# Turning fourteen far tiles of a fused attention backward by DMA, in fixed tiles

## The chip, the cores and the metric

The kernel runs on one core of a Trainium2 chip. The metric is the time of one execution of the whole program in microseconds of the device. Of the core's engines five appear below: TensorE (PE) multiplies matrices and turns (transposes) tiles, VectorE (DVE), ScalarE (ACT) and GpSimd (POOL) work on elements, and SyncE (SP) here does nothing but issue DMA transfers. Each engine works through its own list of instructions in order, and they wait for one another by semaphores.

## The reference: a gated mix of attention and a gated FFN, forward and backward

For a sequence x of 2048 tokens of width 512 the reference computes

```python
g = sigmoid((x * gate_w).sum(-1, keepdims=True))
a = attention(x, wqkv, wo)          # 32 heads of 16, causal, window of 256 keys
b = reglu_ffn(x, W_gate, W_up, W_down)   # inner width 1376
out = g * a + (1 - g) * b
```

and the gradients of `out` against a given `grad_out`, with respect to x as the attention and the gate see it, wqkv, wo, the three FFN weights and gate_w. The input of the FFN is a constant of its own for the gradient. In attention a query i sees the keys k with 0 <= i - k < 256: with tokens cut into blocks of 128, the queries of block j meet the key blocks j (diagonal, cut by the causal mask), j-1 (whole) and j-2 (cut by the far edge of the window). Everything is in bf16, with sums in float32.

## The kernel before

**Stages.** The FFN comes first, forward and backward (to about 249 us). Then comes attention, forward and backward together, in four head groups c = 0 to 3 of eight heads each; in the profiled execution they start at about 249, 351, 467 and 583 us. The output stage follows from about 713 us: a loop over 16 token tiles that makes b (`bps`, L1030) and dwo, and from 767 us a second loop over the 16 tiles that makes a (`aps`, L1064), out and dx (`dxps`, L1055 and L1085).

**A unit of attention.** A head group has 16 rows j (128 queries each). A row has up to three key blocks: "d" (block j), "m" (j-1) and "f" (far, j-2), and each is done in two halves of four heads. So a full row has six units, in the order m, f, d for half 0 and m, d, f for half 1, and the whole has 360. A unit goes through these steps:

- `front`: scores `ST` (L688, keys on the partitions, 128x512), the exp on ACT (L697) into `Pu`, and for d and f a mask on POOL (L699, L702);
- `front_dp`: `dPT` (L711), the product of V and the incoming gradient;
- `gradp`: `Pd = Pu * dPT` on DVE (L716);
- `rowsum`: 8 matmuls (L725, L727) that sum outputs, row sums and dQ of the row in one PSUM tile `BA`;
- `flip`: `Pu` and `Pd` turned, so that queries lie on the partitions, 8 blocks of 128x128;
- `cd_piece`: 8 matmuls (L542, L545) from the turned tile into `CD`, the dK and dV of one key block; when the last piece of a key block is in, ACT copies `CD` out (L548).

**Two ways to turn.** For d and m the two halves share a tile (`PPd`, `PPm`, three buffers each) and are turned together by one DMA transpose of 16 blocks on SP (L744) into `p2d` or `p2m`. The far units are turned one by one by 8 PE transposes (L754) into PSUM, from where ACT (L72) or DVE (L74) copies them into SBUF, by turns. The far tiles `Pu` and `Pd` have two buffers each, the turned ones four.

**The order of work.** One loop over slots n writes the instructions of all engines, and each engine keeps that order. Slot n does `front` of unit n, `front_dp` of unit n-1, `gradp` of unit n-2, the DMA turning of unit n-3 where there is one, and with LAG = 4 `rowsum` of unit n-4 and its PE turning. Pieces of `CD` stand in a queue `cdq` with the slot from which they may go: n+1 for earlier rows, n+5 for the newest row. A credit, refilled each slot and lowered by what PE is given, lets background work in: the projections Q, K, V, dO of the next four rows (`project_parts`, whose `rows` are one 8-block DMA transpose, L181), and the weight gradient of the head group before (`grad_parts`: four parts of four steps of four matmuls, L642; each part's result is stored by SP). All four parts of a head group are released at row 3 of the next one.

**Late turns.** The output stage needs wqkv, W_gate and W_up turned. `turns` cuts them into DMA transposes of up to 8 blocks on SP (L582). They go into slots of SBUF that earlier work has left: x0 to x3, d0 to d3, p0 to p3, each 128 x 4 x 512; p0 to p3 held the projection weights of the four head groups. The table `plan` says after which group of projections which turns may go; they then leave a list `late` one at a time, in head groups 1 and 2 at the slots with n % 12 == 1 in rows 3 to 8. What is in `W_rest` goes in the output stage: four at its start, and then one at each pair of token tiles of the `bps` loop. In the seventh pair `load_wo` and `load_b(0)` follow on SP: W_o, `dgT_g`, `duT_g` and the DMA transpose `turned` (L840), which `aps` reads. `clear` zeroes, on POOL, the 32 rows of a last weight tile that the weight doesn't fill.

Of the kernel before, what the change touches and what calls it, by code (L numbers as in the profile page):

```python
# [11 lines left out]
BF = mybir.dt.bfloat16  # L12
# [10 lines left out]
def kernel(  # L23
# [74 lines left out]
    def slot(tag):  # L98
        return big.tile([P, DC, TGW], BF, tag=tag, name=tag)
# [415 lines left out]
    if True:  # L515
# [68 lines left out]
        def clear(name):  # L584
            nc.gpsimd.memset(W6[(name, FC - 1)][0:FC * P - F, :], 0.0)
# [8 lines left out]
        def turns(name, src, k0, k1, tag):  # L594
            full, end = src.shape[1] // P, -(-src.shape[1] // P)
            ks = range(k0, min(k1, full))
            sets = [list(ks[i:i + 2]) for i in range(0, len(ks), 2)] + ([[full]] if k0 <= full < min(k1, end) else [])
            return [lambda s=s: turn_w(name, src, s, tag, s[0] - k0) for s in sets]
# [19 lines left out]
        def load_gw():  # L618
            nc.sync.dma_start(gw_b[:], gate_w.partition_broadcast(P))

        plan = {2: [load_gw], 5: turns("wqkv", A_wqkv, 0, 4, "p0"), 7: turns("wqkv", A_wqkv, 4, 8, "p1"),
                11: turns("wqkv", A_wqkv, 8, 12, "p2"),
                12: turns("Wg", B_W_gate, 0, 4, "x0") + turns("Wg", B_W_gate, 4, 8, "d0"),
                13: loads("Wd", B_W_down, 0, "x1") + loads("Wd", B_W_down, 4, "d1"), 14: loads("Wd", B_W_down, 8, "x2")}
        W_rest = (turns("Wg", B_W_gate, 8, 12, "d2") + [lambda: clear("Wg")] + turns("Wu", B_W_up, 0, 4, "x3") + turns("Wu", B_W_up, 4, 8, "d3")
                  + turns("Wu", B_W_up, 8, 12, "p3") + [lambda: clear("Wu")])

        def grad_parts(c, tail=False):
            out = []
# [26 lines left out]
                    out.append((lambda part=part, t0=t0, f=(t0 == 0), l=(t0 + 4 == NT): piece(part, t0, f, l), t0 + 4 < NT))  # L656
            return out

        class Unit:
            pass  # L660

        units = []
        for c in range(DC):
            for j in range(NT):
                kbs = [k for k in (j - 1, j, j - 2) if k >= 0]
                for half in range(2):
                    order = kbs if half or len(kbs) < 3 else [kbs[0], kbs[2], kbs[1]]
                    for ki, kb in enumerate(order):
                        u = Unit()
                        u.c, u.j, u.kb, u.half = c, j, kb, half  # L670
                        u.first = ki == 0 and half == 0
                        u.last = ki == len(kbs) - 1 and half == 1
                        u.role = ("d", "m", "f")[j - kb]
                        u.pair = u.role == "d" or (u.role == "m" and (c < DC - 1 or j < NT - 2))
                        u.own = u.role == "f"
                        u.dma = u.pair
                        units.append(u)
        NU = len(units)

        pairs = {}  # L680

        def front(u):
            tg, jl = u.j // TPG, u.j % TPG
            z = zt[(u.c * NTG + tg) % ZB]
            KTt = proj[(u.c, u.kb // TPG)][f"K{u.half}"]
            ksl = slice((u.kb % TPG) * P, (u.kb % TPG + 1) * P)
            ST = ps.tile([P, HH, P], F32, tag="M", bufs=4, name="ST")
            nc.tensor.matmul(ST[:], lhsT=KTt[:, ksl], rhs=z[:, 0, :, jl, :], start=True, stop=True)  # L688
            if not u.own:
                if u.half == 0:  # L690
                    tag = f"PP{u.role}"
                    pairs[(u.c, u.j, u.kb)] = wk.tile([P, 2, 2, HH, P], BF, tag=tag, bufs=3, name=tag)
                u.PP = pairs[(u.c, u.j, u.kb)][:, u.half, :, :, :]
                u.Pu, u.Pd = u.PP[:, 0, :, :], u.PP[:, 1, :, :]
            else:
                u.Pu = wk.tile([P, HH, P], BF, tag="Pu", bufs=2, name="Pu")
            nc.scalar.activation(u.Pu[:], ST[:], ACT.Exp)  # L697
            if u.role == "d":
                nc.gpsimd.affine_select(out=u.Pu[:], in_=u.Pu[:], compare_op=ALU.is_ge, fill=0.0, base=0,  # L699
                                        pattern=[[0, HH], [1, P]], channel_multiplier=-1)  # L700
            elif u.role == "f":
                nc.gpsimd.affine_select(out=u.Pu[:], in_=u.Pu[:], compare_op=ALU.is_ge, fill=0.0, base=-1,  # L702
                                        pattern=[[0, HH], [-1, P]], channel_multiplier=1)
# [7 lines left out]
            nc.tensor.matmul(u.dPT[:], lhsT=VTt[:, ksl], rhs=z[:, 1, :, jl, :], start=True, stop=True)  # L711

        def gradp(u):
            if u.own:
                u.Pd = wk.tile([P, HH, P], BF, tag="Pd", bufs=2, name="Pd")
            nc.vector.tensor_tensor(out=u.Pd[:], in0=u.Pu[:], in1=u.dPT[:], op=ALU.mult)  # L716

        def rowsum(u):
# [17 lines left out]
        def flip(u):  # L736
            key = (u.c, u.j, u.kb, "p2")
            if u.role != "f" and key not in P2 and not (u.pair and u.half == 0):
                P2[key] = wk.tile([P, 2, 2, HH, P], BF, tag=f"P2{u.role}", bufs=3, name=f"p2{u.role}")
            if u.dma:  # L740
                if u.pair and u.half == 0:
                    return
                hs = slice(0, 2) if u.pair else slice(u.half, u.half + 1)
                nc.sync.dma_start_transpose(out=P2[key][:, hs, :, :, :].rearrange("p b a h q -> p (b a h) q"),  # L744
                                            in_=pairs[(u.c, u.j, u.kb)][:, hs, :, :, :].rearrange("p b a h q -> p (b a h q)"))
                for b in range(2)[hs]:
                    P2[(u.c, u.j, u.kb, b)] = P2[key][:, b, :, :, :]
                return
            eng = ("act", "dve", "act")[copier["i"] % 3] if u.c == 0 else ("act", "dve")[copier["i"] % 2]
            copier["i"] += 1  # L750
            pt = psr.tile([P, 2, HH, P], BF, tag="TR", name="pt")
            for a, src in enumerate((u.Pu, u.Pd)):
                for hh in range(HH):
                    nc.tensor.transpose(pt[:, a, hh, :], src[:, hh, :], ident[:])  # L754
            p2 = P2[key][:, u.half, :, :, :] if u.role == "m" else wk.tile([P, 2, HH, P], BF, tag="P2f", bufs=4, name="p2")[:]
            evac(p2, pt[:], eng)
            P2[(u.c, u.j, u.kb, u.half)] = p2

# [84 lines left out]
        with tc.manual_schedule():  # L843
# [36 lines left out]
            while n <= NU + LAG or ev or cdq or bgq:  # L880
                now = ev.pop(n, [])
                u = units[n] if n < NU else None
                if u is not None:
                    gi = u.c * NTG + u.j // TPG
                    if u.first and u.j == 0:
                        sts[u.c] = st.tile([P, NT, 4, P], BF, tag="rows_st", name="rows_st")
                    if u.first and u.j % TPG == 0:
                        if gi + 1 < len(groups):
                            prq = project_parts(*groups[gi + 1]) if gi else second
                            due = n + sum(2 * min(3, j + 1) for j in range(u.j, u.j + TPG)) - 3  # L890
                            if gi + 2 == len(groups):
                                due -= 10
                    if u.first and u.j == TPG and ends:
                        copies.append(ends.pop(0))
                    if u.first and u.j == 1 and u.c > 0:
                        ready = grad_parts(u.c - 1)
                    if u.first and u.j == TPG - 1 and u.c > 0:
                        bgq += ready
                    front(u)
                    if u.last and gi + 1 == len(groups) and u.j % TPG in (1, 3):  # L900
                        ev.setdefault(n + 2, []).append(("dma", (lambda: load_a(0)) if u.j % TPG == 3 else lambda: load_h(0)))
# [18 lines left out]
                if w is not None:  # L920
                    rowsum(w)
                    if not w.dma:
                        flip(w)
                    if w.last:
                        for s, eng, f in small_ops(w.c, w.j, n - 2):
                            ev.setdefault(s, []).append((eng, f))
                        done = [w.j - 2] if w.j >= 2 else []
                        if w.j == NT - 1:
                            done += [NT - 2, NT - 1]
                        for kb in done:  # L930
                            qbs = range(kb, min(NT, kb + 3))
                            for qb in qbs:
                                for half in range(2):
                                    e = n + (1 if qb < w.j else 5)
                                    cdq.append((e, w.c, kb, qb, half, qb == qbs[-1] and half == 1))
                if v is not None and not (w is not None and w.first):
                    front_dp(v)
# [29 lines left out]
                if u is not None and u.c == DC - 1 and not bgq and u.j > 6 and "grads" not in S2:  # L967
                    S2["grads"] = grad_parts(DC - 1, True)
                calm = not NU - 8 < n < NU + 3
                if late and calm and (u is None or u.c == 0 or (n % 12 == 1 and 3 <= u.j <= 8 if u.c < DC - 1 else  # L970
                                                       n % 4 == 1 and 1 < u.j < 10 or n % 2 and u.j > 9)):
                    late.pop(0)()
                credit = max(-1.0, min(1.2, credit))
# [179 lines left out]
```

## Time and profile before

| | us |
|---|---|
| median of 3 runs (lowest to highest) | 905.12 (904.67 to 905.77) |
| the profiled execution | 905.65 |
| its span, first to last instruction | 903.9 |
| attention, head groups 0 / 1 / 2 / 3 | 101.9 / 115.5 / 115.9 / 130.4 |
| output stage, first / second loop | 54.0 / 136.9 |
| busy: PE / DVE / POOL / ACT | 884.3 / 510.0 / 493.7 / 445.6 |

The profile takes one execution. Its span runs from the first to the last instruction. "Busy" counts the time in which an engine had at least one instruction running. The granted TensorE clock was 0.999 of full speed. Lines of a timeline give the start, the duration, the engine and the line of the kernel, and the operation with its output and inputs by the program's names; on an engine's queue (SPq) the duration is the time that the issue of a DMA took, and its landing is a later event. PE's matmuls overlap, so the distance between starts is what one costs. The chain of waits follows the work that ended last back to what released each step. The three kinds of turnings in numbers: 928 PE transposes (L754), 122 DMA transposes of pairs (L744), 16 of `rows` (L181).

### The profile page before, as it was taken

The numbers are of one execution on the slowest core, as the hardware profiler recorded it, in microseconds if no ns is written. First come the engines' busy times: TensorE is split into PE (matmuls) and PEld (weight loads), VectorE is DVE, ScalarE is ACT, GpSimd is POOL, SyncE is SP. The second block draws the span as 40 slices with busy tenths as digits, with TensorE's granted clock in tenths as the row PEclk, the third lists the DMA queues.
The fourth block names the chain that finished last, engine by engine and source line by source line (L and its number), as shares of the span: only waits on it lengthen the run. The fifth ranks groups of instructions, "written<-read, shape, count | busy, mean of one in ns | idle before, by whom it ended". The sixth has DMA issues, their size and how long they took to land.

```text
span 903.9 us, 25852 instructions
## 1 busy us (share of the span) xinstructions
PE 884.3 (98%) x10507; PEld 560.5 (62%) x10607; DVE 510.0 (56%) x946; ACT 445.6 (49%) x787; POOL 493.7 (55%) x937
## 2 busy tenths in 40 slices
PE   8999999999989999999999999999999999999998
PEld 5556656555657777667776677766767644444445
DVE  4433344335368887678886778876777101333343
ACT  6422232222278777667776677766778212111111
POOL 4644445445267778767877577876678200222232
PEclk9999999999999999999999999999999999999999
DMA  9988889999789999999999989999999999998930
GB/s 302 202 191 190 192 181 214 212 215 214 191 138 159 189 184 192 186 176 156 179 181 185 186 161 187 177 198 181 212 178 189 243 248 220 268 273 225 206 117 30
DMA packets 520983, 174.57 MB, mean 193 GB/s; under 512 B 446816, under 2 KB 519744, under 8 KB 520864
## 3 DMA queue, kind: packets, MB, share of 16 engines
q1 hardware_dynamic: 498624, 150.62, 89.6%
q10 hardware_dynamic: 20608, 17.70, 7.2%
q0 software_dynamic: 1632, 4.59, 1.5%
q8 instruction: 83, 1.36, 0.6%
q14 instruction: 36, 0.29, 0.1%
HBM read 34.37 MB, written 36.24 MB: 78 GB/s over the span
## 4 chain that ended last, share of the span: by engine, by line
PE 83%; DVE 5%; DMA 4%; ACT 3%; issue 2%; POOL 2%; SPq 1%; ACTq 0%; POOLq 0%; DVEq 0%
PE dxps L1055 8%; PE ST L688 7%; PE dPT L711 7%; PE wps L412 7%; PE pt L754 5%; PE wps L642 5%; PE dxps L1085 4%; PE bps L1030 4%; PE CD L542 4%; PE BA L725 4%; PE dhps L363 4%; PE pp L133 3%; PE gps L363 3%; PE dps L414 3%; PE ups L363 3%; PE CD L545 3%
## 5 line engine op out<-in xcount | busy, mean ns | idle before, releaser
L688 PE MATMUL ST<-z,K 128*128 128x512 bf16 x360 | 135.8, 378 | 4.5 <-ACT PPd L697 1.3
L711 PE MATMUL dPT<-z,V 128*128 128x512 bf16 x360 | 135.9, 378 | 1.9 <-DVE Pd L716 0.6
L699 POOL TENSOR_SCALAR_AFFINE_SELECT PPd<-PPd 128x512 bf16<-128x512 bf16 x128 | 81.7, 639 | 80.6 <-ACT PPd L697 80.3
L377 POOL TENSOR_TENSOR hT<-rg,upm 128x512 bf16<-128x512 bf16 x44 | 51.7, 1175 | 113.5 <-DVE upm L375 96.8
L412 PE MATMUL wps<-dgu_r,x_r 128*128 128x256 bf16 (+1 forms) x704 | 103.9, 270 | 1.4 <-DVE wst L74 0.6
L716 DVE TENSOR_TENSOR PPd<-PPd,dPT 128x512 bf16<-128x512 bf16 x128 | 86.9, 679 | 20.5 <-PE dPT L711 12.9
L702 POOL TENSOR_SCALAR_AFFINE_SELECT Pu<-Pu 128x512 bf16<-128x512 bf16 x112 | 72.3, 646 | 34.9 <-ACT Pu L697 33.8
L697 ACT ACTIVATE PPd<-ST 128x512 bf16<-128x512 f32 x128 | 77.0, 603 | 24.6 <-PE ST L688 18.7
L716 DVE TENSOR_TENSOR Pd<-Pu,dPT 128x512 bf16<-128x512 bf16 x112 | 76.4, 682 | 21.2 <-PE dPT L711 11.0
L412 PEld LDWEIGHTS <-x_r 128*128 128x128 bf16 x704 | 68.4, 98 | 31.7 <-issue 1.1
L697 ACT ACTIVATE Pu<-ST 128x512 bf16<-128x512 f32 x112 | 67.4, 602 | 37.0 <-PE ST L688 36.8
L716 DVE TENSOR_TENSOR PPm<-PPm,dPT 128x512 bf16<-128x512 bf16 x120 | 80.1, 667 | 7.1 <-PE dPT L711 5.9
L697 ACT ACTIVATE PPm<-ST 128x512 bf16<-128x512 f32 x120 | 72.4, 603 | 16.8 <-PE ST L688 16.3
L375 DVE SCALAR_TENSOR_TENSOR upm<-rg,ups 128x512 bf16<-128x512 bf16 x44 | 30.1, 685 | 80.0 <-PE ups L363 38.7
L369 ACT ACTIVATE rg<-gps 128x512 bf16<-128x512 f32 x44 | 26.3, 598 | 88.0 <-PE gps L363 47.9
L1067 ACT COPY a_sb<-aps 128x512 f32<-128x512 f32 x16 | 9.4, 586 | 107.2 <-issue 99.8
L72 ACT COPY p<-pt 128x1024 bf16<-128x1024 bf16 x59 | 60.1, 1019 | 4.2
L414 PE MATMUL dps<-db_r,h_r 128*128 128x512 bf16 x159 | 60.3, 379 | 0.0
L387 POOL TENSOR_TENSOR dgu<-dh_sb,rg 128x512 bf16<-128x512 bf16 x44 | 57.2, 1301 | 5.3 <-ACT dh_sb L383 5.3
L642 PE MATMUL wps<-rows_st,x_r 128*128 128x384 bf16 x256 | 50.3, 325 | 0.0
L386 DVE TENSOR_TENSOR dgu<-dh_sb,upm 128x512 bf16<-128x512 bf16 x44 | 32.4, 737 | 27.4 <-ACT dh_sb L383 25.2
L133 PE MATMUL pp<-x,p 128*128 128x512 bf16 x152 | 44.4, 378 | 1.9
(179 smaller groups left out, 2315.9 us busy)
## 6 DMA issues: line engine op xcount, KB each, us to landing
dqkvo_d<-rows_st SPq DMA_DIRECT2D x15, 512.0 KB, 3.8
hT_d<-hT ACTq DMA_DIRECT2D x44, 128.0 KB, 2.7
dgT_d<-dgu ACTq DMA_DIRECT2D x44, 128.0 KB, 3.0
duT_d<-dgu ACTq DMA_DIRECT2D x44, 128.0 KB, 3.0
h<-hT_d SPq DMA_DIRECT2D x8, 640.0 KB, 5.7
dgT_g<-dgT_d SPq DMA_DIRECT2D x8, 640.0 KB, 5.5
duT_g<-duT_d SPq DMA_DIRECT2D x8, 640.0 KB, 6.5
go_g<-in_grad_out_dram SPq DMA_DIRECT2D x16, 256.0 KB, 4.9
```

What stands on the lines that cost most here:

```text
L133: nc.tensor.matmul(pp[:], lhsT=w_p[c][:, cd, which * P:(which + 1) * P], rhs=x_T[tg][:, cd, :], start=(cd == 0), stop=(cd == DC - 1))
L363: nc.tensor.matmul(out[:], lhsT=w(c), rhs=x(c), start=(c == 0), stop=(c == DC - 1))
L412: nc.tensor.matmul(acc["w"][:, c, 0:2 * nw], lhsT=x_r[:, t, c * P:(c + 1) * P], rhs=k.dgu_r[:, :, i, s0:P], start=(go_ and c % 2 == 0), st ...
L414: nc.tensor.matmul(acc["d"][:], lhsT=k.h_r[:, i, :], rhs=db_r[:, t, :], start=go_, stop=no_)
L642: nc.tensor.matmul(wps[:], lhsT=x_r[:, t, part * P:(part + 1) * P], rhs=sts[c][:, t, 0:3, :], start=first and t == t0, stop=last and t == ...
L688: nc.tensor.matmul(ST[:], lhsT=KTt[:, ksl], rhs=z[:, 0, :, jl, :], start=True, stop=True)
L697: nc.scalar.activation(u.Pu[:], ST[:], ACT.Exp)
L699: nc.gpsimd.affine_select(out=u.Pu[:], in_=u.Pu[:], compare_op=ALU.is_ge, fill=0.0, base=0, pattern=[[0, HH], [1, P]], channel_multiplier=-1)
L702: nc.gpsimd.affine_select(out=u.Pu[:], in_=u.Pu[:], compare_op=ALU.is_ge, fill=0.0, base=-1, pattern=[[0, HH], [-1, P]], channel_multiplier=1)
L711: nc.tensor.matmul(u.dPT[:], lhsT=VTt[:, ksl], rhs=z[:, 1, :, jl, :], start=True, stop=True)
L716: nc.vector.tensor_tensor(out=u.Pd[:], in0=u.Pu[:], in1=u.dPT[:], op=ALU.mult)
L1055: nc.tensor.matmul(to, lhsT=src[:, fc, lsl], rhs=W6[(wt, fc)][:, cols], start=(fc == 0 and wt == "Wg"), stop=False)
```

## The change

- Fourteen far units, those of half 0 in rows 3, 4, 5, 6, 8, 9 and 10 of head groups 1 and 2, are turned by a DMA transpose of 8 blocks on SP, issued like the pairs in slot n+3, instead of by PE.
- For that, `Pu` and `Pd` of every far unit now lie in one tile `PF`. The far tiles are eight in fixed assignment by row and half: `PF` (two) and `P2F` (four, turned), and in head groups 1 and 2 one more of each in the slot p0.
- Since p0 is in use for longer, the two turns of the first wqkv columns into it move from the plan (after projection group 5) to the end of `W_rest`, so to the output stage. `clear("Wu")` becomes part of the last turn of W_up.
- In head groups 1 and 2 the `CD` pieces of the newest row may go from slot n+7 on, not n+5.
- In head groups 1 and 2 one part of the weight gradient is released at each of the rows 3, 6, 10 and 14.
- In head groups 1 and 2 the late turns go at the first unit of rows 7 and 11.

```diff
-        plan = {2: [load_gw], 5: turns("wqkv", A_wqkv, 0, 4, "p0"), 7: turns("wqkv", A_wqkv, 4, 8, "p1"),
+        plan = {2: [load_gw], 7: turns("wqkv", A_wqkv, 4, 8, "p1"),
...
-                  + turns("Wu", B_W_up, 8, 12, "p3") + [lambda: clear("Wu")])
+                  + turns("Wu", B_W_up, 8, 12, "p3"))
+        W_rest[-1] = lambda last=W_rest[-1]: (last(), clear("Wu"))
+        W_rest += turns("wqkv", A_wqkv, 0, 4, "p0")
...
+        FARC = (1, 2)
...
-                        u.dma = u.pair
+                        u.far = u.own and half == 0 and c in FARC and j in (3, 4, 5, 6, 8, 9, 10)
+                        u.dma = u.pair or u.far
...
+        PF = [wk.tile([P, 2, HH, P], BF, tag=f"PF{i}", bufs=1, name="PF")[:] for i in range(2)]
+        P2F = [wk.tile([P, 2, HH, P], BF, tag=f"P2f{i}", bufs=1, name="p2f")[:] for i in range(4)]
+        far = {}
+
+        def far_tile(u, turned):
+            if u.c not in FARC:
+                return P2F[(2 * u.j + u.half) % 4] if turned else PF[u.half]
+            if not far:
+                x = slot("p0")[:].rearrange("p k n -> p (k n)")
+                far["x"] = [x[:, i * 1024:(i + 1) * 1024].rearrange("p (a h q) -> p a h q", a=2, h=HH) for i in range(2)]
+            if not turned:
+                return PF[1] if u.half else (PF[0], far["x"][0])[u.j % 2]
+            return P2F[2 + u.j % 2] if u.half else (P2F[0], P2F[1], far["x"][1])[u.j % 3]
...
-                u.Pu = wk.tile([P, HH, P], BF, tag="Pu", bufs=2, name="Pu")
+                u.PP = far_tile(u, False)
+                u.Pu, u.Pd = u.PP[:, 0, :, :], u.PP[:, 1, :, :]
...
+            if u.far:
+                P2[(u.c, u.j, u.kb, u.half)] = p2 = far_tile(u, True)
+                nc.sync.dma_start_transpose(out=p2.rearrange("p a h q -> p (a h) q"),
+                                            in_=u.PP.rearrange("p a h q -> p (a h q)"))
+                return
...
-            p2 = P2[key][:, u.half, :, :, :] if u.role == "m" else wk.tile([P, 2, HH, P], BF, tag="P2f", bufs=4, name="p2")[:]
+            p2 = P2[key][:, u.half, :, :, :] if u.role == "m" else far_tile(u, True)
...
-                    if u.first and u.j == TPG - 1 and u.c > 0:
+                    if u.first and u.c in FARC and u.j in (3, 6, 10, 14):
+                        bgq += ready[:NT // 4]
+                        del ready[:NT // 4]
+                    if u.first and u.c > FARC[-1] and u.j == TPG - 1:
                         bgq += ready
...
-                                    e = n + (1 if qb < w.j else 5)
+                                    e = n + (1 if qb < w.j else 7 if w.c in FARC else 5)
...
-                if late and calm and (u is None or u.c == 0 or (n % 12 == 1 and 3 <= u.j <= 8 if u.c < DC - 1 else
+                if late and calm and (u is None or u.c == 0 or (u.first and u.j in (7, 11) if u.c < DC - 1 else
```

More of the change, by code (lines that the diff above doesn't have):

```diff
@@ L713, in gradp @@
         def gradp(u):
-            if u.own:
-                u.Pd = wk.tile([P, HH, P], BF, tag="Pd", bufs=2, name="Pd")
             nc.vector.tensor_tensor(out=u.Pd[:], in0=u.Pu[:], in1=u.dPT[:], op=ALU.mult)
```

## The prediction
> **What bounds the kernel now.** I read the page first, then TensorE's groups and timeline, then SyncE's (SP) timeline, then the chain of waits in the last attention head group, and last the hand-over to the output stage.
>
> The page:
>
> ```profile
> PE 884.3 (98%) x10507; PEld 560.5 (62%) x10607; DVE 510.0 (56%) x946; ACT 445.6 (49%) x787; POOL 493.7 (55%) x937
> ...
> q1 hardware_dynamic: 498624, 150.62, 89.6%
> ...
> PE 83%; DVE 5%; DMA 4%; ACT 3%; issue 2%; POOL 2%; SPq 1%; ACTq 0%; POOLq 0%; DVEq 0%
> ```
>
> TensorE is the bound nearly everywhere, and SP's queue (q1) is busy 89.6% of the span. So a saving on PE counts in full only while the queue, which is to do the work instead, has room.
>
> What one turning on PE costs, in the timeline (start, duration, instruction):
>
> ```profile
> 402.39 0.38 PE L754 MATMUL pt<-ident,Pu 128*128 128x128 bf16 x4
> 402.61 0.39 PE L754 MATMUL pt<-ident,Pd 128*128 128x128 bf16 x4
> 402.83 0.38 PE L711 MATMUL dPT<-z,V 128*128 128x512 bf16 x1
> ```
>
> The matmuls overlap, so starts count: eight transposes hold PE from 402.39 to 402.83, 0.44 us, with the next matmul right behind.
>
> SP's timeline, first where the queue has room, then where it has none:
>
> ```profile
> 402.49 1.68 SPq L744 DMA_TRANSPOSE p2m<-PPm  x1
> 404.27 2.76 SPq L744 DMA_TRANSPOSE p2d<-PPd  x1
> 410.79 1.93 SPq L744 DMA_TRANSPOSE p2m<-PPm  x1
> ...
> 609.61 1.29 SPq L582 DMA_TRANSPOSE x<-in_B_W_gate_dram  x1
> 611.00 2.99 SPq L744 DMA_TRANSPOSE p2m<-PPm  x1
> ...
> 682.79 3.34 SPq L744 DMA_TRANSPOSE p2d<-PPd  x1
> 686.30 3.06 SPq L744 DMA_TRANSPOSE p2m<-PPm  x1
> 689.46 2.42 SPq L744 DMA_TRANSPOSE p2d<-PPd  x1
> ```
>
> An issue into an empty queue takes 1.68 us; behind others it is held to about 3. From 407.03 to 410.79 SP has nothing to do. After 565 it has no pause over 0.85 us until 672.
>
> The chain of waits in the last head group, 664 to 680 us:
>
> ```profile
> 670.04 6.32 DMA p2d<-PPd
> 676.39 0.04 issue
> 676.44 0.12 ACT PPd L697
> ```
>
> Here the queue is already the bound: an exp waits for the tile that a late turning still reads, and PE waits for the exp.
>
> The hand-over to the output stage, PE's and SP's timelines:
>
> ```profile
> 764.61 5.48 SPq L840 DMA_TRANSPOSE turned<-dqkvo_d  x1
> ...
> 771.71 0.81 PE L1055 MATMUL dxps<-p,duT_g 128*128 128x512 bf16 x3
> 772.36 0.59 PE L1064 MATMUL aps<-wo_z,turned 128*128 128x512 bf16 x2
> ```
>
> `turned` lands 7.5 us after its issue, at 772.15, and its first reader starts 0.2 us late on it: no slack.
>
> **The change, part by part.**
>
> *1. Fourteen turnings leave PE.* 14 x 0.44 = 6.2 us less PE work, while PE is the bound. Their copies out of PSUM go too, seven on ACT (1.02 us) and seven on DVE (0.69); both engines are under 60% busy, so I count nothing.
>
> *2. They enter SP's queue.* Each is a transpose of eight blocks, the shape of `rows` (L181, 1.26 us of issue, 3.3 us to landing). What matters is what it takes from a full queue. Eight-block turnings in the backlog space out at 1.39 us (609.61 to 611.00). Half of a sixteen-block pair gives more: four pairs from 686.30 to 698.11 are 2.95 us each, half 1.48. I take the middle, 1.43; the bounds are 1.35 (the 1.26 and SP's 0.1 between issues) and 1.5.
>
> *3. Six turns of wqkv move.* The two of p0 leave head group 1 for the output stage. One of p1 goes from group 2 to row 11 of group 1, one of p2 from group 3 to row 11 of group 2. So ahead of the wait at 676 the queue gets 14 - 2 = 12 more eight-block turnings, 12 x 1.43 = 17.2 us (16.2 to 18.0).
>
> *4. What room the queue has.* Between 351 (start of group 1) and 672, SP pauses eleven times for over 0.85 us, 27.9 us together: 1.5, 1.6, 2.4, 3.8, 3.1, 3.1, 0.9, 1.5, 3.2, 3.6, 3.2. That is the upper bound. The lower counts only pauses with nothing in flight, from the last landing to the next issue (409.59 to 410.79 in the fence above): 3.7 us. The engines can take the next work before a landing is reported: a pair alone lands in 4.3 us and costs 2.95, so 1.4 us of it is not work. Counting from landing less 1.4 gives 14 us, which I take.
>
> *5. The sum in attention.* The queue is first in, first out, and the transfer issued at 670.04 stands at its end. If all its room is used, that transfer lands 17.2 - 14 = 3.2 us later, and PE cannot pass the exp that waits for it. PE alone would gain 6.2. The later of the two decides: +3.2, where about 9.4 us of new waits in groups 1 to 3 eat the 6.2 and go beyond.
>
> *6. Gradient pieces.* The 64 matmuls of 0.162 us per group are spread over rows 3, 6, 10 and 14 in groups 1 and 2; the four stores of `ws` (0.55 us of SP each) move with them. No work is added: zero for PE and queue, since all still stands ahead of 676. The cover is PE itself; if it waits for the queue, moving them gains nothing either.
>
> *7. Far pieces two slots later (5 to 7).* The CD bank's copy (0.37 us on ACT) then has one slot before the next CD block: scores 0.22, sums 0.20 and dPT 0.22 with the sums of the slot before, 0.84 us, against 0.2 of delay and 0.37 of copy. That fits, except where ACT copies a turning (1.02) and BAs (0.50) just before and PE has nothing else between: by the loop's rules two rows, about 0.4 us each. It counts only if PE is the bound: 0 to 0.8; I take 0, since PE then waits for the queue.
>
> *8. Fixed tiles.* PF and P2F have the sizes of the Pu, Pd and P2f they replace. Two more pairs lie in p0, free since group 0 ended. A far tile is written again two rows later, some 11 us after it is ready; a landing takes 4, so SP may be 6 to 7 us behind. It is up to 5.1 now in groups 1 and 2, 10.6 in group 3. No price of its own; it is one of the places where term 5 shows.
>
> *9. Output stage.* W_rest now ends with the two p0 turns. The clear of Wu rides on the turn before, where POOL waits for a landing with nothing behind it. The second p0 turn is issued at the seventh pair of token tiles, directly ahead of wo, dgT_g, duT_g and `turned`. It holds SP and the engines 1.4 us, so `turned` lands 1.4 later, and PE waits. Bounds 0 (SP had 0.38 us idle at 758.15) and 1.9 (the longest such issue). The first p0 turn falls in a pause of 1.8 us: zero; without that pause it would delay a load of h that has 1.8 us in hand.
>
> *Sum.* The profiled execution took 905.65 us (span 903.9 and 1.75 around it), 0.53 above the median. 905.65 + 3.2 + 1.4 = 910.25, against the median 909.7.
>
> **A rule against the row.** A pair carries 524,288 bytes; at 2.95 us this queue moves 178 GB/s. The Trainium skill, "DMA: Bandwidth & Descriptors", section "Latency and other measured facts", gives a DMA transpose 261 GB/s even in its poorer case. By that an estimate is 2.0 us a pair and 1.0 us a far turning, the queue would have tens of us to spare, and the sum would be 900.3. The trace does not agree: 2.95 us is measured where nothing else is queued.
>
> **The rivals.**
>
> *Full gain (faster).* The queue keeps up and PE stays the bound: 905.12 - 6.2 + 1.4 = 900.3, to 901.1 with part 7. It decides this way if the queue's room is at least 17.2 + 6.2 = 23.4 us. For it: SP's pauses sum to 27.9, and in group 1 SP falls back to 0.06 us behind in several rows. Against: after the pause at 446 the next pair is held 3.27 us at once, so the engines were not idle. The Trainium skill's rate above is this case.
>
> *In between.* Room of 16 to 23 us: 901 to 907. For it: the spread of the gradients shortens rows where SP now pauses, and lengthens rows where it lags.
>
> *Deeper backlog (slower still).* A pair costs more when the queue never drains: the landings from 685.54 to 697.96 are 3.1 us apart. Some 75 pair-equivalents stand between 351 and 676; 0.1 us more on most of them is 5 to 7 us, so 915 to 917. Against: with 2.83 us a pair between 468 and 501, where SP also lags, the price is not settled upward.
>
> **How the numbers follow.** Forecast case (room 10 to 16 us, 906 to 914) 0.52; full gain 0.22; in between 0.15; deeper backlog 0.11. A measurement here tells about 0.2%, 1.8 us. Faster: 0.22 and half of "in between", with little from the forecast case: 0.31. Same: 0.11. Slower: 0.58. The range 900.9 to 914.0 leaves out the deeper backlog and under half of the full gain.
>
> **What would show it.** L754's transposes fall from 928 to 816, and fourteen new transposes stand on SP. Term 5 is right if ACT's exps wait for DMA some 9 us in groups 1 to 3 (2.5 now) and SP has hardly a pause over 1 us from 370 to 680. It is wrong if groups 1 and 2 each start some 3 us closer and PE shows no new wait. Part 9 is right if the first reader of `turned` waits about 1.6 us for it.

## The result and the profile after

| | before | after |
|---|---|---|
| median of 7 runs each, on one chip (lowest to highest) | 905.6 us (904.67 to 907.19) | 912.26 us (907.91 to 912.87) |
| profiled span | 903.9 | 910.5 |
| attention, head groups 1 / 2 / 3 | 115.5 / 115.9 / 133.2 | 113.3 / 118.5 / 137.0 |
| output stage, first / second loop | 51.8 / 136.3 | 52.3 / 138.3 |

The change made the kernel slower: the ratio is 1.0050, 95% interval 1.0031 to 1.0070, or 4.5 us on 905.6. The medians stand 6.7 apart, a ratio of 1.0074, which lies above that interval, so the size of the loss is known only to some 2 us. Here and below a head group's time is the distance between the first score matmuls of two groups, and group 3 ends at the first `bps` matmul.

The page of the changed kernel, the same lines as before:

```profile
PE 886.7 (97%) x10495; PEld 554.8 (61%) x10495; DVE 504.3 (55%) x939; ACT 435.0 (48%) x780; POOL 491.5 (54%) x937
...
q1 hardware_dynamic: 513408, 154.29, 93.3%
...
PE 82%; DMA 7%; ACT 3%; SPq 3%; DVE 2%; POOL 2%; issue 1%; ACTq 0%; DVEq 0%; POOLq 0%
```

PE has 112 transposes less, and its busy time has not fallen (in groups 1 to 3 alone it went from 356.9 to 355.7). SP's queue rose from 89.6 to 93.3% of the span, and DMA and SP's queue together hold 10% of the chain, not 5%.

SP's timeline in the stretch of group 1 that had pauses:

```profile
399.03 1.48 SPq L759 DMA_TRANSPOSE p2f<-PF  x1
400.62 3.10 SPq L766 DMA_TRANSPOSE p2m<-PPm  x1
403.83 1.91 SPq L766 DMA_TRANSPOSE p2d<-PPd  x1
405.84 3.99 SPq L766 DMA_TRANSPOSE p2m<-PPm  x1
409.93 2.01 SPq L766 DMA_TRANSPOSE p2d<-PPd  x1
```

Each issue begins 0.1 us after the one before. SP's pauses of over 0.3 us in groups 1 and 2 came to 28.4 us before; now they come to 0.5.

What PE first feels of that, in this profile, is in group 2 (chain of waits, 535 to 560 us):

```profile
533.29 5.59 DMA p<-PF
...
538.97 0.60 ACT PF L716
...
542.52 4.99 DMA p2f<-p
...
547.59 0.60 ACT p L716
```

An exp of row 10 waits for a far tile that the turning of row 8 still reads (`p` is the far tile in slot p0), and PE waits for the exp. Then the last group, row 10, in the chain from 655 to 672 us:

```profile
662.78 6.37 DMA p2m<-PPm
...
669.20 0.19 PE CD L542
```

PE stood 2.73 us for this tile: here it is the reader of the turned tile that is late, not an exp. ACT's waits for DMA in attention, before and then after (total, times, longest):

```profile
ACT PPd L697 <- DMA p2d<-PPd: 2.5, 2, 2.3
```

```profile
ACT PPd L716 <- DMA p2d<-PPd: 7.2, 5, 2.3
ACT PF L716 <- DMA p<-PF: 3.0, 1, 3.0
ACT p L716 <- DMA p2f<-p: 2.2, 1, 2.2
ACT PF L716 <- DMA p2f<-PF: 1.9, 1, 1.9
```

2.5 us became 14.3. How late SP runs is seen best as its lag: from the end of the DVE product that completes a d pair to the issue of its turning. The largest lag in groups 1, 2 and 3 was 4.7, 5.1 and 10.6 us before; it is 9.2, 11.4 and 12.1 after. The gain on PE is there at first, but it is small. Row 10 of group 2 starts 7.8 us earlier than before, counted from the start of group 1; in e1 below, which has the rest of the change and no far turning by DMA, it starts 6.3 us earlier too, because gradient steps now come later. So the far turnings have gained 1.5 us by then. Behind row 10 come the waits above, and by the start of group 3 the changed kernel is 0.3 us behind the kernel before and 1.9 behind e1.

The hand-over, on SP and on PE:

```profile
762.39 1.70 SPq L582 DMA_TRANSPOSE p<-in_A_wqkv_dram  x1
...
770.69 5.43 SPq L862 DMA_TRANSPOSE turned<-dqkvo_d  x1
```

```profile
776.29 0.81 PE L1080 MATMUL dxps<-p,duT_g 128*128 128x512 bf16 x3
778.26 0.60 PE L1089 MATMUL aps<-wo_z,turned 128*128 128x512 bf16 x2 [1.17 <-DMA turned<-dqkvo_d]
```

The reader of `turned` waits 1.17 us, where it had started 0.2 us late.

### The profile page after: what moved, and what is told of

The parts are those of the page before. It is cut to its first block, busy times and chain, and to the rows that moved or that the text cites. A ratio compares the mean times of both kernels' runs of the same rounds, so it can differ in the third digit from the quotient of the medians.

```text
span 910.5 us, 25755 instructions
## 1 busy us (share of the span) xinstructions
PE 886.7 (97%) x10495; PEld 554.8 (61%) x10495; DVE 504.3 (55%) x939; ACT 435.0 (48%) x780; POOL 491.5 (54%) x937
## 3 DMA queue, kind: packets, MB, share of 16 engines
q1 hardware_dynamic: 513408, 154.29, 93.3%
## 4 chain that ended last, share of the span: by engine, by line
PE 82%; DMA 7%; ACT 3%; SPq 3%; DVE 2%; POOL 2%; issue 1%; ACTq 0%; DVEq 0%; POOLq 0%
PE wps L412 8%; PE dPT L730 7%; PE ST L706 7%; PE dxps L1080 7%; PE wps L644 4%; PE pt L776 4%; PE dhps L363 4%; PE gps L363 4%; PE dps L414 4%; PE ups L363 4%; PE CD L542 4%; PE pp L133 4%; PE dxps L1110 4%; PE BA L742 4%; PE bps L1055 3%; PE CD L545 2%
## 5 line engine op out<-in xcount | busy, mean ns | idle before, releaser
L706 PE MATMUL ST<-z,K 128*128 128x512 bf16 x360 | 136.3, 379 | 3.3 <-ACT PPd L716 1.3
L721 POOL TENSOR_SCALAR_AFFINE_SELECT PF<-PF 128x512 bf16<-128x512 bf16 x98 | 63.0, 643 | 30.2 <-ACT PF L716 28.4
L733 DVE TENSOR_TENSOR PF<-PF,dPT 128x512 bf16<-128x512 bf16 x98 | 66.7, 680 | 21.2 <-PE dPT L730 10.3
L716 ACT ACTIVATE PF<-ST 128x512 bf16<-128x512 f32 x98 | 59.8, 610 | 33.5 <-PE ST L706 26.2
L414 PE MATMUL dps<-db_r,h_r 128*128 128x512 bf16 x176 | 66.7, 379 | 0.0
L776 PE MATMUL pt<-ident,PF 128*128 128x128 bf16 x720 | 55.0, 219 | 0.0
L72 ACT COPY p2f<-pt 128x1024 bf16<-128x1024 bf16 x49 | 50.3, 1027 | 1.7
```

Source lines behind the costliest of these rows:

```text
L414: nc.tensor.matmul(acc["d"][:], lhsT=k.h_r[:, i, :], rhs=db_r[:, t, :], start=go_, stop=no_)
```

## The experiments

All times are of the profiled execution, in us; "pauses" are SP's over 0.3 us in groups 1 and 2. The ratio is to runs of the kernel before on the same chip (medians 906.2 to 906.6, and 905.6 for the changed kernel), with its 95% interval.

| kernel | far units by DMA | groups 1 / 2 / 3 | output stage | pauses | ratio |
|---|---|---|---|---|---|
| before | 0 | 115.5 / 115.9 / 133.2 | 188.1 | 28.4 | 1 |
| after | 14 | 113.3 / 118.5 / 137.0 | 190.7 | 0.5 | 1.0050 (1.0031 to 1.0070) |
| e1_no_far | 0 | 114.7 / 115.1 / 129.9 | 190.8 | 30.7 | 0.9981 (0.9965 to 0.9997) |
| e2_pe_too | 14, on PE too | 115.1 / 116.5 / 133.5 | 194.3 | 3.9 | 1.0048 (1.0030 to 1.0067) |
| e3_group1 | 7 | 113.3 / 117.4 / 131.2 | 189.9 | 12.2 | 1.0000 (0.9987 to 1.0014) |
| e4_p0_last | 14 | 114.8 / 117.3 / 136.5 | 189.3 | 0.5 | 1.0044 (1.0029 to 1.0059) |
| e5_group1_turns_kept | 7 | 114.2 / 115.3 / 133.3 | 190.5 | 8.6 | 0.9987 (0.9972 to 1.0002) |
| e6_g1_kept_p0_last | 7 | 114.1 / 115.2 / 133.8 | 189.8 | 9.4 | 0.9985 (0.9969 to 1.0002) |
| e7_p0_back | 0 | 114.7 / 115.1 / 132.2 | 188.1 | 29.1 | 0.9977 (0.9964 to 0.9990) |
| e8_two_m_on_pe | 14 | 113.3 / 117.8 / 133.0 | 190.5 | 0.4 | 1.0011 (0.9997 to 1.0024) |
| e9_p0_back_one_m_on_pe | 0 | 114.7 / 115.1 / 133.3 | 189.5 | 29.4 | 0.9963 (0.9948 to 0.9977) |
| e10_eight_far | 8 | 113.7 / 114.1 / 132.5 | 190.3 | 9.6 | 0.9990 (0.9977 to 1.0003) |

One caution for the whole table: group 3 can come out some 3 us longer or shorter from nearly the same start. e1 and e5, whose code for this group is the same, enter it with the same lag (1.8 us in row 0, 7.8 and 7.7 in row 2), but in e5 a pair of row 7 holds SP for 5.42 us (4.31 in e1), the lag is 2 to 3 us higher from there to row 11, and the group ends 3.4 us later. So group 3 of one profile is a hint, and the ratios decide.

**e1: no far unit by DMA, all the rest kept.**

```diff
-                        u.far = u.own and half == 0 and c in FARC and j in (3, 4, 5, 6, 8, 9, 10)
+                        u.far = u.own and half == 0 and c == -1
```

> The changed kernel with no far unit turned by DMA; all the rest of the change stays (fixed tiles, later gradient pieces, spread gradient steps, moved wqkv turns). Queue theory: the debt of SP's queue is gone (12 eight-block turnings fewer ahead of the last attention group's waits than in the changed kernel), PE does its 928 transposes again, so attention takes what it took before and the output stage keeps its loss: 905.6 + 1.9 for the output stage, up to 0.8 for the later pieces, so 907 to 908.5; SP pauses of over 0.3 us come back (28 us in groups 1 and 2, 0.5 in the changed kernel). Rival, the rest of the change is what costs: stays at 911 or more, and would reach 918 if the far turnings themselves had gained their 6.2.

It came out below the kernel before, at 0.9981, and so outside both expectations. The pauses are back, and no far or d tile makes ACT wait in attention. In the page's chain PE has 89%, where the changed kernel has 82:

```profile
PE 89%; DVE 3%; DMA 3%; ACT 2%; issue 1%; POOL 1%; SPq 0%; ACTq 0%; DVEq 0%; POOLq 0%
```

So the fourteen turnings alone are worth 1.0050 - 0.9981 = 0.0069, or +6.2 us (7.7 by the medians; the two intervals leave about 2 us either way), and the rest of the change is a gain, which neither theory had.

**e2: the fourteen units turned on PE as well.**

```diff
                     if not w.dma:
                         flip(w)
+                    elif w.far:
+                        pt = psr.tile([P, 2, HH, P], BF, tag="TR", name="pt")
+                        for a, src in enumerate((w.Pu, w.Pd)):
+                            for hh in range(HH):
+                                nc.tensor.transpose(pt[:, a, hh, :], src[:, hh, :], ident[:])
```

> The changed kernel, and the fourteen far units are turned on PE as well (eight transposes each into a PSUM tile that nobody reads), so the 6.2 us of PE work are back while the queue's work stays. Queue theory: the wait in row 10 of the last group comes when the queue has worked off its list, so PE's extra work falls into time in which PE waited: 0 to +2.5 us on the changed kernel's 912.3 (912 to 915), with less waiting on DMA in groups 2 and 3. Rival, PE is still the bound in most of attention: +5 to +6, so 917 to 918.5.

6.2 us of PE work put back cost nothing: 1.0048 against 1.0050, where the rival needed some 1.0105 or more. So over the whole of attention PE is not the bound of the changed kernel, and the rival falls. Group 1, where neither PE nor ACT waits for the queue yet, became 1.8 us longer, and groups 2 and 3 became 2.0 and 3.5 shorter. Together they even took 3.6 us less in this profile (365.1 against 368.7), with lags of 5.8, 10.2 and 11.3; the output stage took 3.6 more, in waits for loads. With the caution above I can't say whether the 3.6 us are more than the spread.

Group 1 also shows what a turning is worth on PE. The two kernels give PE the same order of work there, but for 56 transposes, 3.1 us, and PE has no wait of over 0.25 us in the changed one; still they are 1.8 us apart, not 3.1. Of the seven slots that lost their transposes three became 0.44 to 0.45 us shorter, and four 0.07 to 0.33; two later slots became 0.2 longer. What PE waits for in those places, mostly for too short to be listed, was not followed up.

**e3 and e5: only the seven units of group 1.** e3 restricts the far units to c == 1. In e5 the counter that alternates the copies out of PSUM between ACT and DVE is set on by one more after the seven.

```diff
+                copier["i"] += u.j == 10
                 P2[(u.c, u.j, u.kb, u.half)] = p2 = far_tile(u, True)
```

> The changed kernel with only the seven far units of head group 1 turned by DMA. Queue theory: the queue gets 5 net eight-block turnings (7.2 us) ahead of the last group's wait, less than its room of 12 to 14 us, so it has caught up in group 2: group 1 keeps its 2.3 us, group 2 is as before to 0.5, group 3 as before, the output stage loses 1.9: 905.6 - 2.3 + 1.9 = 905.2 (904.5 to 906.5). If the cost went evenly with the number of turnings (half of the way from no far turning to all fourteen): 909.5 to 910.5. If the far tiles are too few (waits of the exp for a tile that is still being read), group 1 shows none, as in the changed kernel, and the time is the same as by the queue theory.

> As e3_group1, but the alternation of the copies out of PSUM between ACT and DVE is set on by one more after the seven turnings taken off PE, so that every later far unit has the engine that it had in e1_no_far (in e3 seven is odd and all later ones swap). Theory: the 2.3 us that e3's group 2 lost against e1 (117.4 against 115.1) and the 1.3 of its group 3 are the swap, not the queue: group 1 at 113.3, group 2 at 115.1 to 115.5, group 3 at 130, so 2 to 3.5 us less than e3: a ratio of 0.996 to 0.998 to before. Rival, those 3.6 us are the queue's debt of group 1: no difference from e3 (1.000).

Against e1, e3 gained 1.4 us in group 1 and lost 2.3 in group 2, which the queue theory had not expected. The cause is first seen on ACT at the start of group 2, in e3 and then in e5:

```profile
470.96 0.60 ACT L716 ACTIVATE PPd<-ST 128x512 bf16<-128x512 f32 x1 [1.57 <-DMA p2d<-PPd]
471.46 0.49 ACT L748 COPY BAs<-BA 128x400 f32<-128x400 f32 x1
471.83 1.03 ACT L72 COPY p2f<-pt 128x1024 bf16<-128x1024 bf16 x1
```

```profile
471.64 0.60 ACT L716 ACTIVATE PPd<-ST 128x512 bf16<-128x512 f32 x1 [1.63 <-DMA p2d<-PPd]
472.13 0.49 ACT L748 COPY BAs<-BA 128x400 f32<-128x400 f32 x1
472.50 0.61 ACT L716 ACTIVATE PPm<-ST 128x512 bf16<-128x512 f32 x1
```

Both come out of a wait for a pair of group 1. In e3 a far copy of 1.03 us stands on ACT between there and the next exp, because an odd number of turnings taken off PE swapped ACT and DVE for all that followed. With the alternation restored group 2 takes 115.3, e1's 115.1: the expectation for group 2 is met. Group 1 missed it (114.2, not 113.3): in row 12 an exp waits 2.3 us for a far tile that is still being read, and PE 1.1 us for the exp, as in e4 and e6. Group 3 missed it too (133.3, not 130), as in the caution. The ratio, 0.9987, lies above the 0.996 to 0.998 expected, and it overlaps with e3's, so in total the swap stays within the error.

The changed kernel carries the same swap from the start of group 2 until that group's own seven turnings make the number even. Its lead over e1 falls from 1.5 us at the start of group 2 to 0.7 at row 4 and is back at 1.5 at row 10. So most of what it loses in group 2 comes after that, at the waits for far tiles, where PE stands 3.4 us; but no run has fourteen turnings without the swap, and a part of the 6.2 us may be the swap's. What e3 and e5 say together: seven turnings bring nothing against none (0.9987 and 1.0000 against 0.9981), though PE has 3.1 us less to do.

**e4 and e6: the second p0 turn behind the first loads of the last loop**, in the changed kernel and in e5.

```diff
-                    if W_rest:
+                    if W_rest and g < NG - 2:
                         W_rest.pop(0)()
                     if g == NG - 2:
                         load_wo()
                         grp_next = load_b(0)
+                        W_rest.pop(0)()
```

> The changed kernel with the second wqkv turn into p0 issued behind the loads and turnings of the first pair of tiles of the last loop, not ahead of them. Queue theory of the output stage: the turned tile lands 1.4 us earlier, and its first reader's wait (1.2 to 1.3 us) goes: -1.0 to -1.4, unless wqkv's columns are then late for their own readers (-0.3 to 0). If the loss in the last loop (2.0 us) has another cause, no difference. Attention as in the changed kernel.

> e5, and the second wqkv turn into p0 behind the first loads of the last loop as in e4. If both theories hold, e5's time less 0.8 to 1.4 us: 0.995 to 0.997 of before, ahead of both kernels. If the hand-over's loss is not the place of that turn: the same as e5.

The reader of `turned` no longer waits in e4. PE's waits for DMA in e4's last loop are these instead:

```profile
PE dxps L1081 <- DMA duT_g<-duT_d: 0.5, 1, 0.5
PE dxps L1081 <- DMA dgT_g<-dgT_d: 0.2, 1, 0.2
```

The turn's 1.4 us now delay the loads of the next pair of tiles. The last loop went from 138.3 to 137.5, not to before's 136.3; in e6 it took 138.0, in e5 137.9. Neither ratio moved by more than its error, and e6, at 0.9985, is not in the 0.995 to 0.997 expected. The gain of 0.8 to 1.4 us was not found.

**e7: e1 with the two p0 turns back in group 1**, and no far tile in p0.

```diff
-        plan = {2: [load_gw], 7: turns("wqkv", A_wqkv, 4, 8, "p1"),
+        plan = {2: [load_gw], 5: turns("wqkv", A_wqkv, 0, 4, "p0"), 7: turns("wqkv", A_wqkv, 4, 8, "p1"),
...
-        W_rest += turns("wqkv", A_wqkv, 0, 4, "p0")
+        W_rest += []
...
-            if u.c not in FARC:
+            if True:
```

> e1_no_far with the two wqkv turns into p0 back in head group 1 (no far unit turned by DMA, no far tile in p0). Theory: SP's queue was in debt in the last head group already before the change, and the two turns (2 x 1.43 = 2.9 us) moved out of attention are what made e1's group 3 3.2 us shorter than before (129.9 against 133.2): here group 3 is back at 132 to 133.5, and the output stage back at 188 (190.7 in e1): -2.5 there, +3 in attention, so within 1 us of e1 in all. Rival, group 3's gain in e1 came from the spread gradients, the later pieces or the tiles: group 3 stays at 130 and the time falls by 2.5.

The output stage is back at 188.1 to the tenth, group 3 at 132.2, and the total within 0.4 us of e1 (0.9977 against 0.9981): as expected. ACT waits again for a late pair:

```profile
ACT PPd L716 <- DMA p2d<-PPd: 2.2, 1, 2.2
```

So moving the two turns is neutral: what attention gains the output stage pays. And e7 is the kernel before with only the gradient steps, the later pieces, the rows of the late turns and the fixed tiles: these are worth -0.0023, or 2.1 us, outside the interval. Which of them does it was not separated; PE's idle time in groups 1 and 2 fell from 2.9 to 2.1 us.

**e8: two m pairs of group 3 on PE, in the changed kernel; e9: one, in e7.**

```diff
-                        u.pair = u.role == "d" or (u.role == "m" and (c < DC - 1 or j < NT - 2))
+                        u.pair = u.role == "d" or (u.role == "m" and (c < DC - 1 or j < NT - 2 and j not in (3, 6)))
```

(e9 has `j != 3` in that place.)

> The changed kernel, with the m pairs of rows 3 and 6 of the last head group turned on PE (four more times eight transposes) and not by DMA. Queue theory: 5.9 us less in the queue ahead of the wait in row 10, which took 2.9 us, and of the waits in rows 11 and 14; PE pays 4 x 0.44 = 1.8. Net -2 to -4 on the changed kernel, so about +1 to +2.5 on before, with group 3 at 133 to 135 (137.0). Rival, PE is the bound: +1.8.

> e7_p0_back, and the m pair of row 3 of the last head group turned on PE, not by DMA: the opposite of the change, at the place where the queue is in debt. Queue theory: 2.95 us less in the queue, where e7's group 3 still waits about 1.9 us for late turnings (rows 11 and 12) and 0.85 in row 5; PE pays 2 x 0.44 = 0.9. Group 3 at 130 to 131.3 (132.2 in e7), so 0.995 to 0.997 of before. Rival, PE is the bound there: +0.9, 0.9985.

In e8 1.8 us more work on PE made the kernel 3.5 us faster (1.0011 against 1.0050, with intervals that do not overlap), in the range expected; group 3 went from 137.0 to 133.0, and its waits in rows 10 to 14 are gone. e9, which does the opposite of the change, is the fastest of all, at 0.9963, 902.93 us against 906.17: ahead of both kernels. That its 0.0014 over e7 are the queue's is not shown: the intervals overlap, and in the profile, which was the slowest of its executions, group 3 takes 133.3, where 130 to 131.3 were expected.

**e10: eight far units, in rows 3, 4, 8 and 9.**

```diff
+                        u.far = u.own and half == 0 and c in FARC and j in (3, 4, 8, 9)
```

> The changed kernel with eight far units by DMA, half 0 of rows 3, 4, 8 and 9 of head groups 1 and 2: each far tile is then written again only after four or five rows, so the wait of an exp for a far tile still being read can't come up, and the count taken off PE is even in each group. Queue theory: 8 x 1.40 = 11.2 us more in the queue than in e1_no_far; from 0, 7 and 14 turnings (attention 359.8, 362.8, 368.7) attention comes to 362.5 to 365, 0.998 to 1.001 of before, with waits for p2m and p2d in the last head group. Rival, the far tiles are what is short (their two-row reuse made the waits of rows 8 to 12 in group 2): those waits go, the 3.5 us of PE work are gained in full, attention 356 to 357.5, 0.994 to 0.996.

No far tile is waited for any more, groups 1 and 2 are each 1.0 us shorter than e1's, and group 3 is 2.5 longer, with PE at two late pairs:

```profile
PE CD L542 <- DMA p2m<-PPm: 2.3, 2, 1.4
```

Attention, 360.3, is shorter than the queue theory's 362.5 to 365 and far from the rival's 356 to 357.5; the ratio, 0.9990, lies in the former's range and outside the latter's. That fits a shortage of far tiles that only set where the queue's lateness first showed; fourteen turnings with more tiles were not run. On PE the eight turnings gained 2.0 us in groups 1 and 2, 0.25 each and not 0.44.

## Why the prediction held, step by step

The forecast was +4.6 us in all with a range of 900.9 to 914.0; the ratio gives +4.5, the medians +6.7. The way and the main mechanism were right: the queue, with less room than the new turnings need, ate what PE gained. That the ratio's figure is so near is luck. By the runs below attention cost 0.8 more than forecast and the output stage 1.2 more, and 2.1 came back from parts that were put at zero; each of these is known to 1 or 2 us.

- **Steps 1 and 5, PE's 6.2 us come to nothing because the queue bounds.** Shown by e2 (work put back, no cost), e8 (work added, time gained) and e1 (turnings away, 6.2 us gained). But the 6.2 us of step 1 were never there in full: where the queue doesn't bind yet, in group 1, seven turnings gained 1.4 us on e1 and 1.8 on e2, not 3.1. And in the last group it is not the exp of step 5 on which PE stands longest, but a reader of the turned tile (2.73 us; 0.7 before). The marks named for it are there: 816 transposes, ACT's waits at 14.3 us (some 9 were forecast), no pause over 1 us between 370 and 680.
- **Step 2, 1.43 us a turning.** It holds as far as the traces tell. Least-squares fits over the stretches of four pairs in which SP never paused, 21 in the changed kernel, give 2.9 to 3.1 us a pair and 1.2 to 1.7 an eight-block turning, by how the stretches are cut; the error of one fit is about 0.08 and 0.2. That is the price before, 2.95, as near as it can be read, but 0.1 us more a pair, which the rival "deeper backlog" asked for, can't be excluded by it. (Its working counted 75 pair-equivalents between 351 and 676; the trace of the kernel before has 85 pairs and 22 turnings of up to eight blocks there, some 96.) The rival falls by its time: it gave 915 to 917, and the slowest of the seven executions took 912.87. The Trainium skill's 261 GB/s ("DMA: Bandwidth & Descriptors", section "Latency and other measured facts") isn't reached in this backlog either: 524,288 bytes in 2.9 to 3.1 us are 169 to 181 GB/s.
- **Steps 3 and 4, 12 turnings against 14 us of room.** At 1.40 us each the 14 turnings cost 19.6 us of queue. They cost 6.2 us of time by the ratios of e1 and after, so the room is 13.4; by the two profiles (attention 359.8 and 368.7) it is 10.7. The 14 taken are just above, and less than half of the 30.7 us of pauses, as argued. By the ratios of e7 and after the loss is 0.0073, 6.6 us; less the 2.6 of the output stage, attention's part is 4.0, where the sum had 3.2.
- **Steps 6 to 8 at zero.** Wrong by 2.1 us to the good (e7). It was argued that moved work gains nothing while PE waits for the queue; but in groups 1 and 2 of the kernel before PE did not wait for it, and e7's groups 1 and 2 are each 0.8 us shorter. Step 7's risk (a CD copy too late) did not come in e7; in the changed kernel `CD` waits for it in groups 1 and 2 for 0.9 us in all, a little over the 0.8 that the step allowed.
- **Step 9, 1.4 us at the hand-over.** The place is right and the size too small: e1 and e7 differ by 2.6 us in the output stage (190.8 and 188.1). The wait for `turned` was 1.2 in e1 and in the changed kernel (some 1.6 were forecast). The rest is shorter waits in both loops, in the changed kernel for loads (`duT_g` 0.4, `h` 0.25), in e1 for a copy on ACT (0.5). The step counted one reader, and a turn also pushes the loads behind it in the queue, as e4 shows.
- **What the working did not have** is the clock, below: about 1.3 us in the profiled execution.

"Full gain" is refuted by e2. "In between" describes e10: eight turnings use up pauses, gain 2.0 us in groups 1 and 2 and give 2.5 back in group 3.

## What to carry to other kernels

Before moving work off a busy engine to a queue, count the queue's work over the whole stage up to the wait that ends it, not over the place where the work is put: here the pauses that took the new transfers were repaid a head group later. The pauses were worth less than half their length as room. What leaves the busy engine can be worth less than its own length, too: a turning of 0.44 us on PE gained 0.2 to 0.26. And where work alternates between engines by a counter, taking an odd number out swaps the engines for everything behind it.

## What was unexpected: half the clock after a wait

The granted clock in windows of 2 us around the wait in row 10 of group 3, in the changed kernel (the columns: window, then busy time and instructions of PE, PEld, DVE, ACT and POOL, then the granted clock, the DMA share and GB/s):

```profile
664.00:666.00 2.00, 2.00 (x46) 1.53 (x44) 1.82 (x4) 1.51 (x4) 1.70 (x5) 1.00 1.15 214
...
670.00:672.00 2.00, 2.00 (x30) 1.14 (x29) 1.38 (x2) 1.45 (x3) 0.67 (x2) 0.71 0.99 202
672.00:674.00 2.00, 2.00 (x35) 1.72 (x34) 0.69 (x1) 1.46 (x4) 1.70 (x4) 0.50 1.25 217
674.00:676.00 2.00, 2.00 (x43) 1.41 (x41) 1.83 (x4) 0.91 (x3) 0.61 (x2) 0.94 0.91 170
```

After 2.73 us without work (666.48 to 669.20) PE ran for 3.4 us, from 670.84 to 674.25, at half the clock. Row 11, in which no wait of over 0.2 us is left, took 7.21 us against 5.90 in e1: 1.3 us are lost on top of the wait. e4 shows the same with a wait of 3.6 us (half the clock for 6.8 us, from within the wait; row 11: 7.62), and e6 after one of 1.6 (0.50 from 688 to 690, row 14 at 7.38 against 6.15). After waits of 1.1 us in the kernel before, 1.5 in e5 (row 13) and 1.7 in e2 (for `turned`) the clock stayed at 1.00. What decides, for waits of 1.5 to 1.7 us, is open. Of the seven executions of the changed kernel five have a mean clock of 0.994 to 0.998 and took 910.4 to 912.9 us; the two at 1.000 took 907.9 and 909.8. Of e7's twelve, one is below 1.000. But the mean doesn't say where the clock fell: e5's 0.998 comes from the first 12 us of the program (0.50 from 8 to 10 us), and six of e1's twelve are below 1.000. So how many of the seven executions lost time in attention this way is not shown. The Trainium skill, "TensorE: Matmul & The Clock Gate", section "HAM oscillation — how this bites in real kernels", warns of idle gaps over about 3.4 us; here a gap of half that was followed by half the clock in one profile (e6) and not in others.
